# Sparse attention with an MLP: another order of the later batches, another start and other banks at the end

## Chip, core and metric

The kernel runs on one core of one Trainium2 chip. The metric is the device time of one execution in microseconds. Most executions of one kernel on one core fall into one state here ("fast"), and only those are compared. TensorE is named PE, VectorE DVE, ScalarE ACT, GpSimd POOL and SyncE SP in the profile; PEld is TensorE's weight load.

## The reference

Four batches, eight heads, 768 positions, head size 64. Scores are masked by blocks of 32 (neighbours, first and last block, three sampled blocks per row), go through a softmax and meet the values; the result, as rows of 512, goes through an MLP with a squared relu.

```python
scores = scale * np.matmul(q, k.transpose(0, 1, 3, 2))
scores = np.where(mask, scores, -1000000000.0)
attn = np.exp(scores - np.max(scores, axis=-1, keepdims=True))
attn = attn / (np.sum(attn, axis=-1, keepdims=True) + 1e-09)
x = np.matmul(attn, v)                  # -> (4*768, 512)
r = np.maximum(x @ w_in, 0.0)           # w_in (512, 2048)
out = (r * r) @ w_out                   # w_out (2048, 512)
```

## The kernel before

Two heads make a "pair", so there are 16 pairs, four per batch. A pair's queries are three tiles of 256, its keys three chunks of 256, so there are 144 pieces ("score slots") of scores, exponential and value products. The MLP goes by tiles of 256 or 384 rows: sixteen hidden products, relu on VectorE or ScalarE, square on GpSimd, then output products.

No engine is programmed by hand. Each piece of work is a `Task` with an engine, an assumed duration, a priority and its dependences, and a list scheduler in Python lays them out before the build. What it decides is only the order of instructions on each engine; on the chip they wait for semaphores.

```python
def run_schedule(free, bufs, ring):          # free: when each engine is assumed to start
    ...
            at = min(c[0] for c in cand)
            t = min((c[1] for c in cand if c[0] <= at + 1e-9), key=lambda t: (t.key, t.order))
    ...
order = [(a, qi, cp) for qi in range(NQ) for a in range(HP) for cp in range(CP)]
order += [(u, qi, cp) for u in range(HP, NU) for qi in range(NQ) for cp in range(CP)]
...
need = [mu[b * HP + a, qi] for a in range(HP)        # a hidden tile needs all four pairs
        for qi in range(c0 // QW, (c0 + w - 1) // QW + 1)]
...
def y_pool(T, ts):                           # PSUM bank of an output tile
    return "h" if T == TILES[-1] and ts % 2 else "y"
...
for _ in range(8):                           # warm-up of TensorE's clock
    nc.tensor.matmul(pw, warm[:, 0:P], warm, start=True, stop=True)
...
land_k = [(4.4, 5.0), (7.3,), (9.6,), (12.2,)]       # assumed landing times of the first loads
...
run_schedule({"PE": 4.4, "DVE": 4.3, "ACT": 3.5, "POOL": 7.5, "SP": 10.5}, ...)
```

The softmax here doesn't subtract the row's maximum and nothing guards it: scores larger than these inputs give would overflow.

## Time and profile before

| | |
|---|---|
| time, median of 3 | 324.03 us (323.83 to 324.04) |
| the profiled execution | 325.12 us, span 323.3 us |
| TensorE busy | 308.5 us, 95% of the span |
| ScalarE / VectorE / GpSimd busy | 227.3 / 204.4 / 178.6 us |
| first hidden product | 39.7 us |
| last matmul starts | 319.06 us |

TensorE is busy nearly all the time, so the kernel can win only where TensorE waits or runs slowly.

### The profile page before, as it was taken

The page shows a single profiled execution, that of the slowest core. Times are in us where ns is not written, and L with a number is a line of the kernel's source. Part 1 is how long each engine was busy: PE and PEld are TensorE (multiplying, and loading weights), DVE is VectorE, ACT ScalarE, POOL GpSimd, SP SyncE. Part 2 cuts the span into 40 slices and gives each one's busy share as a digit, 9 for nine tenths or more (in the row PEclk, how much of TensorE's full clock was granted, in tenths as well). Part 3 has the DMA queues.
Part 4 walks back from the last instruction along what each step waited for, and adds up shares of the span by engine and source line. Part 5 has one row for each costly group of instructions (what it writes and reads, how often), then busy time and mean ns, then how long its engine had stood idle before and what let it go on. Part 6 is the DMA issues. An engine that isn't in the chain of part 4 may idle for free. (4 is left out here: it accounts for less than half of the span.)

```text
span 323.3 us, 6147 instructions
## 1 busy us (share of the span) xinstructions
PE 308.5 (95%) x2333; PEld 173.9 (54%) x2333; DVE 204.4 (63%) x367; ACT 227.3 (70%) x362; POOL 178.6 (55%) x226
## 2 busy tenths in 40 slices
PE   7998899999999998999989998999999999999994
PEld 2654456556555554555555544565656565555541
DVE  7544463487986877598887695877877653232200
ACT  2698988779998988797768788888788863111211
POOL 7560162287775575097997480554545455666620
PEclk9999999999999999999999999999999999999999
DMA  7997199416555734843754712000000000100002
GB/s 245 325 209 169 48 128 185 146 26 203 86 179 160 220 87 152 229 109 120 195 127 126 204 32 71 16 0 34 32 2 32 35 29 35 36 32 32 34 32 97
DMA packets 42453, 34.47 MB, mean 107 GB/s; under 512 B 20664, under 2 KB 39352, under 8 KB 42424
## 3 DMA queue, kind: packets, MB, share of 16 engines
q1 hardware_dynamic: 37656, 29.63, 32.1%
q0 software_dynamic: 4224, 4.19, 7.9%
q8 instruction: 18, 0.29, 0.4%
q10 hardware_dynamic: 544, 0.26, 0.3%
q14 instruction: 11, 0.09, 0.1%
HBM read 27.26 MB, written 6.29 MB: 104 GB/s over the span
## 5 line engine op out<-in xcount | busy, mean ns | idle before, releaser
L437 POOL TENSOR_TENSOR g<-r 128x384 bf16<-128x384 f32 (+1 forms) x144 | 129.4, 908 | 113.0 <-DVE r L431 91.2
L365 ACT ACTIVATE pT<-ps 128x1024 bf16<-128x1024 f32 x144 | 143.2, 1018 | 31.9 <-PE ps L359 23.1
L420 PE MATMUL ph<-xT,w_in_sb 128*128 128x384 bf16 (+1 forms) x576 | 118.5, 309 | 1.0 <-DVE r L431 0.9
L450 PE MATMUL py<-w_out_sb,g 128*128 128x512 bf16 x384 | 109.1, 379 | 1.4 <-ACT ys L455 1.4
L370 DVE TENSOR_TENSOR pT<-pT,mask 128x1024 bf16<-128x1024 bf16 x108 | 89.2, 839 | 18.3 <-ACT pT L365 16.8
L431 DVE TENSOR_SCALAR r<-ph 128x384 f32<-128x384 f32 (+1 forms) x98 | 49.6, 512 | 54.3 <-PE ph L420 42.1
L383 PE MATMUL po<-pT,VA 128*128 128x256 bf16 x288 | 71.9, 276 | 5.6 <-ACT pT L365 3.7
L420 PEld LDWEIGHTS <-w_in_sb 128*128 128x128 bf16 x576 | 53.0, 98 | 44.8 <-issue 11.2
L385 PE MATMUL po<-pT,VB 128*128 128x256 bf16 x288 | 71.4, 274 | 0.0
L450 PEld LDWEIGHTS <-g 128*128 128x128 bf16 x384 | 37.1, 98 | 25.3 <-issue 2.5
L359 PE MATMUL ps<-QT,KT 64*128 64x256 bf16 x576 | 50.6, 275 | 0.0
L383 PEld LDWEIGHTS <-VA 128*128 128x128 bf16 x288 | 28.2, 98 | 29.7 <-issue 15.4
L429 ACT ACTIVATE r<-ph 128x384 f32<-128x384 f32 (+1 forms) x46 | 20.7, 450 | 27.7 <-POOL g L437 20.2
L359 PEld LDWEIGHTS <-KT 64*128 64x128 bf16 x576 | 22.6, 95 | 21.6 <-issue 19.4
L385 PEld LDWEIGHTS <-VB 128*128 128x128 bf16 x288 | 28.4, 98 | 6.3
L455 ACT COPY ys<-py 128x512 f32<-128x512 f32 x24 | 13.9, 584 | 18.5 <-PE py L450 14.8
L403 DVE TENSOR_TENSOR xT<-po,rs 64x256 bf16<-64x256 f32 x48 | 19.8, 413 | 11.3 <-ACT rs L394 11.2
L392 ACT ACTIVATE ls<-po 64x256 f32<-64x256 f32 x48 | 18.3, 382 | 7.1 <-PE po L385 6.1
L297 POOL CAST qc<-qs 128x768 bf16<-128x768 f32 (+1 forms) x20 | 16.1, 812 | 10.8 <-DMA qs<-in_q_dram 8.4
L394 ACT ACTIVATE rs<-ls 128x256 f32<-128x256 f32 x48 | 20.0, 416 | 1.5
L404 DVE TENSOR_TENSOR xT<-po,rs 64x256 bf16<-64x256 f32 x48 | 20.5, 428 | 0.6
L393 ACT ACTIVATE ls<-po 64x256 f32<-64x256 f32 x48 | 18.1, 376 | 0.6
(49 smaller groups left out, 109.9 us busy)
## 6 DMA issues: line engine op xcount, KB each, us to landing
vs<-in_v_dram SPq DMA_DIRECT2D x16, 384.0 KB, 4.8
out_dram<-ys SPq DMA_DIRECT2D x24, 256.0 KB, 2.0
ks<-in_k_dram SPq DMA_DIRECT2D x15, 384.0 KB, 4.6
qs<-in_q_dram SPq DMA_DIRECT2D x12, 384.0 KB, 3.6
w_in_sb<-in_moe_w_in_dram POOLq DMA_DIRECT2D x4, 512.0 KB, 8.7
w_out_sb<-in_moe_w_out_dram POOLq DMA_DIRECT2D x4, 512.0 KB, 9.4
qs<-in_q_dram SPq DMA_DIRECT2D x11, 128.0 KB, 5.4
ks<-in_k_dram SPq DMA_DIRECT2D x1, 256.0 KB, 2.9
```

The lines of the kernel that those rows point to most:

```text
L359: nc.tensor.matmul(ps[:, h, c, :], KT[i][hs, ksl[c]], QT[i][hs, qsl], start=not add, stop=True, skip_group_check=True)
L365: nc.scalar.activation(out=pT, in_=stile.pop((u, qi, cp)), func=AF.Exp, scale=scale)
L370: eng.tensor_mul(out=pT, in0=pT, in1=mask[:, None, qi, cp * 2:cp * 2 + 2, :].broadcast_to([P, 2, 2, QW]))
L383: nc.tensor.matmul(po[:, 0, :], VA[i][:, n, :], pT[:, 0, c, :], start=first, stop=last, skip_group_check=True)
L385: nc.tensor.matmul(po[:, 1, :], VB[i][:, n, :], pT[:, 1, c, :], start=False, stop=last, skip_group_check=True)
L394: nc.scalar.activation(out=rs, in_=ls, func=AF.Exp, scale=-1.0)
L404: V.tensor_mul(out=xT[b][D:P, a, qsl], in0=po[D:P, 1, :], in1=rs[D:P, :])
L420: nc.tensor.matmul(ph, w_in_sb[:, kc, f * P:(f + 1) * P], xT[b][:, kc, c0:c0 + w], start=(kc == 0), stop=(kc == KM - 1))
L429: nc.scalar.activation(out=r, in_=htile.pop((T, f)), func=AF.Relu)
L431: V.tensor_scalar(out=r, in0=htile.pop((T, f)), scalar1=0.0, scalar2=None, op0=AOP.max)
L437: G.tensor_mul(out=g, in0=r, in1=r)
L450: nc.tensor.matmul(py, gtile[T, f][:, ts * P:(ts + 1) * P], w_out_sb[:, f, :], start=(f == 0), stop=(f == NF - 1))
```

## The change

Three parts are meant to help: the order, the start and the end. In batches 1 to 3, query tiles 0 and 1 of all four pairs come first and tile 2 after, so that a batch's first hidden tile (rows 0 to 383) is ready earlier. At the start, one load goes to another queue, the mask's constants are made in two parts and as 16-bit numbers, and of the eight warm-up matmuls of 512 columns four stay, while ten of 256 columns are put between the first real ones. The last three output tiles get a bank each, and the last one's copy and store are cut in two. With the start, the times that the scheduler assumes change too.

```diff
-    load_part(nc.scalar, 0, 0, 0, 1)
+    load_part(nc.sync, 0, 0, 0, 1)
...
-    for _ in range(8):
-        nc.tensor.matmul(pw, warm[:, 0:P], warm, start=True, stop=True)
+    for _ in range(4):
+        warm_up(512)
...
-    key = consts.tile([P, S], F32, name="key")
+    key = consts.tile([P, S], mybir.dt.int16, name="key")
...
-    one_hot()
+    one_hot(0, 2)
...
-        return "h" if T == TILES[-1] and ts % 2 else "y"
+        return "h" if T == TILES[-1] and ts else "y"
...
+    def out_last(T, ts):
+        py = ytile.pop((T, ts))
+        for eng, queue, half in ((nc.scalar, nc.scalar, 0), (V, nc.sync, 1)):
...
-    land_k = [(4.4, 5.0), (7.3,), (9.6,), (12.2,)]
+    land_k = [(3.0, 4.4), (6.7,), (9.3,), (12.0,)]
...
-    order += [(u, qi, cp) for u in range(HP, NU) for qi in range(NQ) for cp in range(CP)]
+    for b in range(1, B):
+        for qs in (range(NQ - 1), range(NQ - 1, NQ)):
+            order += [(u, qi, cp) for u in range(b * HP, (b + 1) * HP) for qi in qs for cp in range(CP)]
...
+    wu = [Task("PE", 0.2, 1e6, (lambda: warm_up(256)), get=None if i else "po") for i in range(10)]
...
-    run_schedule({"PE": 4.4, "DVE": 4.3, "ACT": 3.5, "POOL": 7.5, "SP": 10.5},
+    run_schedule({"PE": 3.0, "DVE": 3.9, "ACT": 3.2, "POOL": 6.2, "SP": 10.5},
```

More of the change, by code (lines that the diff above doesn't have):

```diff
@@ L218, with warm_up @@
     pw = ps_o.tile([P, 512], F32, name="pw", tag="po")
-    for _ in range(8):
-        nc.tensor.matmul(pw, warm[:, 0:P], warm, start=True, stop=True)
+    def warm_up(n):
+        nc.tensor.matmul(pw[:, 0:n], warm[:, 0:P], warm[:, 0:n], start=True, stop=True)
+    for _ in range(4):
+        warm_up(512)
     HALVES = (slice(0, D), slice(D, P))
-    key = consts.tile([P, S], F32, name="key")
+    key = consts.tile([P, S], mybir.dt.int16, name="key")
     ends = consts.tile([P, 2], F32, name="ends")
@@ L229, with one_hot @@
         G.iota(ends[hs, 0:1], pattern=[[0, 1]], base=0, channel_multiplier=block, **small)
-    G.iota(key, pattern=[[1, NCH], [NCH, P]], base=0, channel_multiplier=0, **small)
+    G.iota(key[:, 0:2 * P], pattern=[[1, 2], [NCH, P]], base=0, channel_multiplier=0, **small)
     identb = consts.tile([P, P], BF, name="identb")
     make_identity(nc, identb)
-    def one_hot():
-        V.tensor_scalar(out=ends[:, 1:2], in0=ends[:, 0:1], scalar1=float(block - 1), scalar2=None, op0=AOP.add)
-        V.tensor_scalar(out=oh, in0=key, scalar1=ends[:, 0:1], scalar2=None, op0=AOP.is_ge)
-        V.scalar_tensor_tensor(out=oh, in0=key, scalar=ends[:, 1:2], in1=oh, op0=AOP.is_le, op1=AOP.mult)
+    G.iota(key[:, 2 * P:S], pattern=[[1, NCH - 2], [NCH, P]], base=2, channel_multiplier=0, **small)
+    def one_hot(n0, n1):
+        cols = slice(n0 * P, n1 * P)
+        V.tensor_scalar(out=oh[:, cols], in0=key[:, cols], scalar1=ends[:, 0:1], scalar2=None, op0=AOP.is_ge)
+        V.scalar_tensor_tensor(out=oh[:, cols], in0=key[:, cols], scalar=ends[:, 1:2], in1=oh[:, cols],
+                               op0=AOP.is_le, op1=AOP.mult)
     sbf = consts.tile([nb, n_rand], F32, name="sbf")
@@ L251 @@
     V.memset(pm[:, 0, nb - 1:nb], 1.0)
-    one_hot()
+    V.tensor_scalar(out=ends[:, 1:2], in0=ends[:, 0:1], scalar1=float(block - 1), scalar2=None, op0=AOP.add)
+    one_hot(0, 2)
+    bm = consts.tile([nb, 2, D], BF, name="bm")
+    V.memset(bm, 0.0)
     V.tensor_copy(out=sbf, in_=sb_i.rearrange("q (r two) -> q r two", two=2)[:, :, 0])
@@ L258 @@
         cur = 1 - cur
-    bm = consts.tile([nb, P], BF, name="bm")
-    V.memset(bm, 0.0)
-    for hs in HALVES:
-        V.tensor_scalar(out=bm[:, hs.start:hs.start + nb], in0=pm[:, cur, :], scalar1=-1.0, scalar2=-NEG,
-                        op0=AOP.add, op1=AOP.mult)
+    V.tensor_scalar(out=bm[:, :, 0:nb], in0=pm[:, cur:cur + 1, :].broadcast_to([nb, 2, nb]), scalar1=-1.0,
+                    scalar2=-NEG, op0=AOP.add, op1=AOP.mult)
     bq = consts.tile([P, S], BF, name="bq")
@@ L271, in rows_product @@
         pb = ps_y.tile([P, QW], F32, name="pb", tag="y")
-        nc.tensor.matmul(pb, bm, oh[0:nb, qi * QW:(qi + 1) * QW], start=True, stop=True)
+        nc.tensor.matmul(pb, bm.rearrange("a t j -> a (t j)"), oh[0:nb, qi * QW:(qi + 1) * QW], start=True, stop=True)
         mtile[qi] = pb
@@ L454, in out_copy @@
         ys = work.tile([P, d_model], F32, name="ys", tag="ys", bufs=3)
-        nc.scalar.copy(out=ys, in_=ytile.pop((T, ts)))
+        py = ytile.pop((T, ts))
         ystile[T, ts] = ys
+        nc.scalar.copy(out=ys, in_=py)
     def store(T, ts):
         nc.sync.dma_start(out=ov[T[0], :, T[1] // P + ts, :], in_=ystile.pop((T, ts)))
+    def out_last(T, ts):
+        py = ytile.pop((T, ts))
+        for eng, queue, half in ((nc.scalar, nc.scalar, 0), (V, nc.sync, 1)):
+            ys = work.tile([P, d_model], F32, name="ys", tag="ys", bufs=3)
+            cols = slice(half * d_model // 2, (half + 1) * d_model // 2)
+            (eng.copy if eng is nc.scalar else eng.tensor_copy)(out=ys[:, cols], in_=py[:, cols])
+            queue.dma_start(out=ov[T[0], :, T[1] // P + ts, cols], in_=ys[:, cols])
     for u in (2, 3):
@@ L475 @@
     K_PARTS = {0: [(0, 1), (1, CP)]}
-    land_k = [(4.4, 5.0), (7.3,), (9.6,), (12.2,)]
-    land_q = [(4.4, 13.8, 15.2), (7.5, 14.1, 15.5), (9.8, 14.5, 15.9), (12.4, 14.8, 16.2)]
-    land_v = [6.2, 8.6, 11.0, 13.4]
+    land_k = [(3.0, 4.4), (6.7,), (9.3,), (12.0,)]
+    land_q = [(3.5, 13.8, 15.3), (7.1, 14.2, 15.7), (9.7, 14.6, 16.1), (12.4, 14.9, 16.5)]
+    land_v = [5.6, 8.2, 10.9, 13.5]
     LAT = 0.08
@@ L490 @@
     wl, tr, gate, mk, tp = {}, {}, [], {}, {HP - 1: []}
+    wu = [Task("PE", 0.2, 1e6, (lambda: warm_up(256)), get=None if i else "po") for i in range(10)]
+    for a, b in zip(wu, wu[1:]):
+        b.deps.append(a)
+    wu[0].bufs[0].holds += 1
+    wu[-1].put.append(wu[0].bufs[0])
+    oh_t = Task("DVE", 1.0, 0.5, (lambda: one_hot(2, NCH)), after=5.6, **SEM)
     rc = []
     for qi in range(NQ):
-        rp = Task("PE", 0.2, -7 + 7 * qi, (lambda qi=qi: rows_product(qi)), get="y", **pe)
-        rc.append(Task("ACT", 0.4, -7 + 7 * qi, (lambda qi=qi: rows_copy(qi)), deps=[rp], put=[rp], **SEM))
+        rp = Task("PE", 0.2, -7 if qi == 0 else 12 * qi - 6, (lambda qi=qi: rows_product(qi)), get="y",
+                  deps=[oh_t] if qi else [], after=7.0 * qi, **pe)
+        rc.append(Task("ACT", 0.4, -7 if qi == 0 else 12 * qi - 6, (lambda qi=qi: rows_copy(qi)), deps=[rp], put=[rp], **SEM))
     for qi in range(NQ):
@@ L559, in attend @@
         sc = Task("PE", 0.42 if len(slots) == 1 and s >= N_FIRST else 0.645, s, (lambda: scores(slots)),
-                  deps=[rc[qi] for u, qi, cp in slots if qi < NQ_ADD and u < HP] + [ev[u][1, cp] for u, qi, cp in slots] + [ev[u][0, qi] for u, qi, cp in slots] + sc_all[-1:],
+                  deps=[t for u, qi, cp in slots if qi < NQ_ADD and u < HP for t in (rc[qi], oh_t)[:1 + (cp > 0)]] + [ev[u][1, cp] for u, qi, cp in slots] + [ev[u][0, qi] for u, qi, cp in slots] + sc_all[-1:],
                   get="ps", n=len(slots), **pe)
@@ L624 @@
                     yhead = yy
-                if part == NY - 1:
+                if part == NY - 1 and T_ == TILES[-1] and last_ts:
+                    Task("ACT", 0.59, 0, (lambda T_=T_, ts=ts: out_last(T_, ts)), deps=[yy], get="ys",
+                         put=[yhead], late=2.0)
+                elif part == NY - 1:
                     yc = Task("ACT", 0.59, 0, (lambda T_=T_, ts=ts: out_copy(T_, ts)), deps=[yy], get="ys",
```

## The prediction

> **What bounds the kernel now.** I read the page's first part, the busy time by stretches, the waits of TensorE after 40 us, and the timeline of both ends. Columns of the stretches: start:end, length, then busy us (and instructions) of PE, PEld, DVE, ACT, POOL, then granted clock, DMA share, GB/s.
>
> ```profile
> PE 308.5 (95%) x2333; PEld 173.9 (54%) x2333; DVE 204.4 (63%) x367; ACT 227.3 (70%) x362; POOL 178.6 (55%) x226
> ...
> 24.00:32.00 8.00, 6.40 (x72) 3.68 (x74) 3.58 (x10) 7.16 (x10) 0.12 (x1) 1.00 0.76 165
> ...
> 120.00:140.00 20.00, 18.52 (x140) 10.10 (x138) 13.44 (x24) 16.57 (x28) 7.09 (x8) 1.00 0.55 165
> ...
> 180.00:200.00 20.00, 18.78 (x139) 10.10 (x134) 14.31 (x24) 16.18 (x26) 9.94 (x10) 1.00 0.38 106
> ...
> 240.00:260.00 20.00, 20.00 (x150) 11.65 (x148) 14.67 (x26) 16.63 (x26) 9.66 (x9) 1.00 0.08 27
> ```
>
> TensorE bounds the kernel from 40 us on and ScalarE before that (7.16 of 8 us at 24 to 32 us, with no hidden-layer matmul yet). TensorE has no room from 220 to 315 us; it starves a little in two stretches, 120 to 140 and 180 to 200 us.
>
> ```profile
> PE po L383 <- ACT pT L365: 1.4, 3, 0.7
> PE po L383 <- DVE xT L404: 1.4, 3, 0.9
> PE ph L420 <- DVE r L431: 0.9, 1, 0.9
> ```
>
> These are only gaps in which no matmul is in flight. From the start times of consecutive matmuls less their streaming time (0.11 us for 256 columns, 0.16 for 384, 0.22 for 512) I count every pause above 0.25 us between 40 and 311 us. The sum is 7.1 us: 2.0 at 122 to 133 us, 1.0 at 164, 2.7 at 191 to 204, the rest in four pauses of 0.3 to 0.4 us before 76 us. The first and third places are where one batch's MLP has only output matmuls left and the next batch's first hidden tile is not ready.
>
> The start, as a timeline (start, length, engine, line, instruction):
>
> ```profile
> 2.33 0.62 DVE L236 TENSOR_SCALAR oh<-key,ends 128x768 bf16<-128x768 f32 x1
> ...
> 2.98 1.02 DVE L237 SCALAR_TENSOR_TENSOR oh<-key,ends,oh 128x768 bf16<-128x768 f32 x1
> ...
> 5.15 0.26 DVE L262 TENSOR_SCALAR bm<-pm 24x24 bf16<-24x24 f32 x2
> ...
> 5.47 0.39 PE L272 MATMUL pb<-oh,bm 24*128 24x256 bf16 x1 [0.69 <-DVE bm L262]
> ...
> 12.48 0.42 PE L383 MATMUL po<-pT,VA 128*128 128x256 bf16 x1
> ...
> 12.69 0.42 PE L385 MATMUL po<-pT,VB 128*128 128x256 bf16 x1
> ...
> 14.17 2.12 ACT L365 ACTIVATE pT<-ps 128x1024 bf16<-128x1024 f32 x2 [1.92 <-PE ps L359]
> ...
> 15.38 0.27 PE L383 MATMUL po<-pT,VA 128*128 128x256 bf16 x1
> ...
> 15.49 0.27 PE L385 MATMUL po<-pT,VB 128*128 128x256 bf16 x1
> ```
>
> Equal matmuls start 0.21 us apart at 12.5 us and 0.11 apart at 15.4: TensorE runs at half rate until about 13.3 us, although the granted-clock column says 1.00. Its slow transposes and value products hold back the fourth exponential to 14.17, ScalarE's last long wait; after that ScalarE has bubbles of only 0.3 us until 40 us. So what the start is worth is read at that fourth exponential.
>
> The end:
>
> ```profile
> 314.70 1.07 ACT L455 COPY ys<-py 128x512 f32<-128x512 f32 x2 [6.33 <-PE py L450]
> 315.83 3.61 PE L450 MATMUL py<-w_out_sb,g 128*128 128x512 bf16 x16 [0.78 <-ACT ys L455]
> ...
> 319.52 0.59 ACT L455 COPY ys<-py 128x512 f32<-128x512 f32 x1 [3.75 <-issue]
> ```
>
> The last output product waits 0.78 us for its PSUM bank; then come copy, store and 3.2 us to the end of the span.
>
> **What the Trainium skill says.** "TensorE: Matmul & The Clock Gate", Part 1: the array runs at half rate by default and goes to full rate after about 3.4 us of sustained work, counted in a free-running window. The trace agrees on the factor (0.21 against 0.11 us). Eight warm-up matmuls of 0.43 us (1.19 to about 4.6 us) plus the gapped work up to 9.9 us did not release it, the dense work of 9.9 to 13.3 us did; that fits windows that end near 6.5, 9.9 and 13.3 us, which is my inference. "DMA: Bandwidth & Descriptors", Issuing engines are not separate DMA queues: issuing from another engine saves only issue time. The trace agrees: the DMA share is 1.04 or more from 3.1 us on, so moving the first query load to the SP queue changes order, not bandwidth. "PSUM — Partial Sum Buffer", Terms: ScalarE and VectorE may not access one bank and quadrant at once. No run shows this yet, but the built program does what it implies: the new VectorE half copy of the last tile waits for ScalarE's half copy.
>
> **Part 1, the start.** The one-hot work ahead of the mask rows falls from 768 to 256 columns. The first compare took 0.62 us; with about 0.15 fixed (the 128x1 instruction before it), a third of the rest gives 0.31. The second took 1.02, 0.2 of it fixed, so about 0.47. That saves 0.31 + 0.55 = 0.85, one write of bm instead of two about 0.13: bm and all casts come about 1.0 us earlier (first product near 4.4 instead of 5.47). But the program order puts six 256-column warm-ups directly behind it: 6 x 0.213 = 1.28 us cold, so the first transposes start near 5.9, as before (5.83). The warm-ups eat this head start. What they buy is a nearly gapless TensorE: following the order with cold durations, three more warm-ups to 7.0, transposes to 7.4, scores, one warm-up, row product, scores to 9.75, that is about 3.1 us streaming of the 3.4 between 6.5 and 9.9, against about 2.6 before. So I expect the full rate at about 9.9 instead of 13.3. Then the first exponential is near 8.5 (8.76 before), the second near 10, third 11, and the fourth, for pair 1, whose keys are cast near 8.4 and transposed at full rate near 9.8, at about 12.1 instead of 14.2. ScalarE is the bound from there, so the gain is carried to 40 us: 2.1 us. If the clock is not released it is only 0.2 to 0.5. I weight these and take **1.8 us**. The second one-hot part (about 0.46 + 0.74 us on VectorE) lies in its wait for transposes and costs the second scores product little.
>
> **Part 2, the order.** Nothing is added: the same 144 score, 144 value, 576 hidden and 384 output pieces; the groups of scores between other matmuls (each costs about 0.2 us of switching, from starts at 59.81, 60.02, 60.34) go from 107 to 108: **+0.2**. A batch's first hidden tile needs query tiles 0 and 1 of four pairs: 8/12 of the batch's attention now, 11/12 before. In the built order hidden matmuls issued by score slot 72, 84, 108, 120 are 188, 212, 320, 350 before and 196, 252, 334, 376 after. The two starved places of before (slots 72 to 84: 24 hidden pieces; 108 to 114: 4) are gone; a shorter one (slots 66 to 72: 6) is new, with eight output pieces to fill it. Of 7.1 us I let 4.7 (both batch boundaries) go, and put 1.0 back for the new place: **3.7 us** gained.
>
> **Part 3, the end.** The third tile gets its own bank: **-0.78**. The last copy, 0.59, becomes ScalarE's half (0.37, as the 128x256 PSUM copy of the mask rows) and, behind it because of the wait, VectorE's half (0.42, as its 128x256 relu) plus about 0.1 for the semaphore: 0.89, so 0.3 later; the half store may land 0.1 to 0.2 sooner (2.0 us for 256 KB). Net **+0.2**.
>
> Sum: 324.03 - 1.8 - 3.7 - 0.78 + 0.2 + 0.2 = 318.1 us, 1.8% less.
>
> **Rivals.** (a) The warm-ups fail: the window's phase is other than inferred, or 92% busy is not enough, and they only delay the transposes. For it: three microseconds of dense warm-up failed before. Then about 319.7. (b) The pauses move rather than go: K and V buffers of a pair now live until the third query tile, there are five, and loads, casts and transposes of the next pairs bunch; or ScalarE limits the runs of scores without hidden work. Against it: a buffer is free at least 15 score slots (about 2 us each) before reuse, and a load plus transpose takes 4.8 + 2.9 us. Then the middle gives 1 us, total about 320.8. (c) The middle becomes gapless: all 7.1 us go with the new place hidden by its output matmuls, and the total is near 314.7. (d) TensorE was the bound anyway and an early start is absorbed: against it, the idle 10% of 24 to 40 us come from ScalarE, and later work follows in the same order.
>
> **Range and chances.** Best case of start and middle together 315, both poor about 321.5. The limit for 2% is 317.55, 0.5 below my number, so faster is a little less likely than not. Nothing adds time worth 2%. Range 315.3 to 321.0; faster 0.40, same 0.59, slower 0.01.
>
> **What would show it.** Right: 256-column matmuls 0.11 us apart from about 10 us; fourth exponential near 12.1; first hidden matmul near 38 instead of 39.7; TensorE busy over 19.3 in each 20 us stretch between 120 and 200 us except one; no wait before the last sixteen output matmuls; the VectorE half copy beginning only after ScalarE's. Wrong: half rate still at 13 us; new pauses on DMA transposes or VectorE in the third-tile passes; more than 3 pauses over 0.5 us after 60 us.

## The result and the profile after

The changed kernel takes 320.65 us (median of 4, 320.05 to 321.18) against 323.98 for before. The ratio is 0.9898 (95% interval 0.988 to 0.9915), 1.0% less time. A ratio here is the mean time of one kernel's fast runs over that of the other's in the same rounds, so not quite the ratio of the medians quoted.

The page's first part and the busy time by stretches, in the columns told in the prediction:

```profile
PE 306.7 (96%) x2339; PEld 174.2 (55%) x2339; DVE 203.3 (64%) x369; ACT 226.7 (71%) x362; POOL 176.9 (55%) x227
...
24.00:32.00 8.00, 7.24 (x79) 4.04 (x78) 3.23 (x7) 7.44 (x11) 0.00 (x0) 1.00 0.69 145
...
120.00:140.00 20.00, 19.34 (x152) 11.00 (x150) 16.66 (x27) 16.04 (x25) 15.82 (x17) 1.00 0.54 153
...
180.00:200.00 20.00, 18.56 (x137) 10.27 (x136) 15.29 (x27) 16.48 (x27) 11.37 (x13) 1.00 0.47 124
```

The first starved stretch is better (19.34 us busy of 20, before 18.52). The second is not (18.56, before 18.78). TensorE's waits after 40 us:

```profile
PE ph L426 <- DVE r L437: 1.6, 4, 0.7
PE po L389 <- ACT pT L371: 0.9, 3, 0.4
PE py L456 <- ACT ys L463: 0.7, 1, 0.7
```

One line of the same view of the kernel before, which the prediction left out, belongs beside the last of these:

```profile
PE py L450 <- ACT ys L455: 1.4, 2, 0.8
```

So output products waited for their bank twice before, at 193 us and at the end; the second of these waits has gone. The wait of hidden products for VectorE's relu has grown from one of 0.9 us to four with 1.6 in total. By the count of the prediction (start times of consecutive matmuls less streaming, pauses above 0.25 us after 40 us), but this time from every single matmul record, pauses went from 6.6 us, plus 0.9 for the last bank, to 5.1. Two of the new kernel's largest, in the timeline (start, length, engine, line, instruction):

```profile
127.88 1.18 DVE L303 CAST qc<-ks 128x768 bf16<-128x768 f32 x1
...
129.09 0.56 DVE L437 TENSOR_SCALAR r<-ph 128x384 f32<-128x384 f32 x1
...
129.71 0.48 PE L426 MATMUL ph<-xT,w_in_sb 128*128 128x384 bf16 x2 [0.66 <-DVE r L437]
...
184.84 0.58 ACT L463 COPY ys<-py 128x512 f32<-128x512 f32 x1 [0.17 <-PE py L456]
...
185.48 1.89 PE L456 MATMUL py<-w_out_sb,g 128*128 128x512 bf16 x8 [0.67 <-ACT ys L463]
```

At 129 us VectorE runs a 1.18 us cast of the next pair's keys before the relu that TensorE needs. At 185 us eight output products wait for a copy out of the one bank that such tiles have in mid-kernel, as they did at 193 us before. The start:

```profile
2.22 0.28 DVE L241 TENSOR_SCALAR oh<-key,ends 128x256 bf16<-128x256 int16 x1
...
2.54 0.48 DVE L242 SCALAR_TENSOR_TENSOR oh<-key,ends,oh 128x256 bf16<-128x256 int16 x1
...
4.20 0.20 DVE L268 TENSOR_SCALAR bm<-pm 24x48 bf16<-24x48 f32 x1
...
4.77 1.46 PE L221 MATMUL pw<-warm 128*128 128x256 bf16 x6
...
11.47 0.27 PE L391 MATMUL po<-pT,VB 128*128 128x256 bf16 x1
...
11.58 0.27 PE L389 MATMUL po<-pT,VA 128*128 128x256 bf16 x1
...
14.08 1.02 ACT L371 ACTIVATE pT<-ps 128x1024 bf16<-128x1024 f32 x1 [0.51 <-PE ps L365]
```

The constants take what the prediction worked out (0.28 and 0.48 us; 0.31 and 0.47 were expected), and equal matmuls are 0.11 us apart by 11.5 us. The fourth exponential starts at 12.55 us, the sixth at 16.25 (before 17.44). The end:

```profile
311.82 1.07 ACT L463 COPY ys<-py 128x512 f32<-128x512 f32 x2 [6.33 <-PE py L456]
315.71 0.37 ACT L474 COPY ys<-py 128x256 f32<-128x256 f32 x1 [2.81 <-issue]
...
316.11 0.42 DVE L474 COPY ys<-py 128x256 f32<-128x256 f32 x1 [10.25 <-ACT ys L474]
```

The bank's wait is gone, and VectorE's half copy starts 0.03 us after ScalarE's has ended.

### The profile page after: what moved, and what is told of

Its sections match the earlier page's. It is cut to its first block, busy times and chain, and to the rows that moved or that the text cites. A ratio compares the mean times of both kernels' runs of the same rounds, so it can differ in the third digit from the quotient of the medians.

```text
span 319.4 us, 6150 instructions
## 1 busy us (share of the span) xinstructions
PE 306.7 (96%) x2339; PEld 174.2 (55%) x2339; DVE 203.3 (64%) x369; ACT 226.7 (71%) x362; POOL 176.9 (55%) x227
## 4 chain that ended last, share of the span: by engine, by line
PE 81%; ACT 9%; DVE 6%; issue 4%; DVEq 0%; ACTq 0%
PE ph L426 24%; PE py L456 22%; PE po L389 11%; PE ps L365 10%; PE po L391 9%; ACT pT L371 5%; PE ps L361 3%; DVE pT L376 2%; DVE r L437 1%; ACT ls L399 1%; ACT ls L398 1%; ACT rs L400 1%; PE pw L221 1%; PE pt L314 1%; DVE xT L410 0%
## 5 line engine op out<-in xcount | busy, mean ns | idle before, releaser
L398 ACT ACTIVATE ls<-po 64x256 f32<-64x256 f32 x48 | 18.2, 380 | 8.6 <-PE po L391 7.6
L463 ACT COPY ys<-py 128x512 f32<-128x512 f32 x23 | 13.3, 584 | 12.7 <-PE py L456 12.7
L303 POOL CAST qc<-qs 128x768 bf16<-128x768 f32 (+1 forms) x20 | 15.2, 771 | 11.8 <-DMA qs<-in_q_dram 10.1
L308 POOL CAST VA<-vs 128x384 bf16<-128x384 f32 x16 | 10.8, 672 | 16.9 <-PE po L389 9.4
```

Of the source, the lines that this page charges most:

```text
L398: nc.scalar.activation(out=ls[0:D, :], in_=po[D:P, 0, :], func=AF.Ln)
```

## The experiments

Twelve kernels ran, each on one chip beside the kernel before. All gave right results. Two measures from the traces help, because the times scatter: the start of the 31st exponential (how well the head of the kernel went) and the stretch from there to the start of the last matmul (how well the rest went). Both are start times read from the trace.

| kernel | median us | ratio to before | full clock from, us | 31st exponential | stretch | span after last start |
|---|---|---|---|---|---|---|
| before, first profile | 323.98 | 1 | 13.6 | 52.5 | 266.6 | 4.28 |
| changed | 320.65 | 0.9898 | 10.3 | 51.5 | 263.8 | 4.16 |
| changed, again | 320.72 | 0.9907 | 10.7 | 51.7 | 263.7 | 4.13 |
| order only | 320.94 | 0.9895 | 4.4 to 7.8, 11.2 | 51.45 | 263.0 | 4.26 |
| start only | 325.3 | 1.0034 | 9.0 | 51.0 | 268.5 | 4.26 |
| end only | 322.77 | 0.9959 | 5.0 to 8.5, 11.9 | 51.4 | 265.4 | 4.13 |
| changed, ten warm-ups out | 320.73 | 0.9892 | 12.0 | 51.7 | 263.8 | 4.14 |
| order and end | 319.24 | 0.9852 | 4.8 to 8.2, 11.7 | 51.3 | 262.1 | 4.12 |
| changed, old planner times | 319.82 | 0.9876 | 10.3 | 52.3 | 262.2 | 4.15 |
| before, new planner times | 325.01 | 1.0038 | 13.0 | 52.2 | 267.4 | 4.26 |
| order and end, again | 319.12 | 0.9851 | 5.1 to 8.5, 11.9 | 51.4 | 262.05 | 4.12 |
| order and end, delay 0.10 | 319.88 | 0.9878 | 13.2 | 52.3 | 262.7 | 4.15 |
| order and end, delay 0.06 | 319.83 | 0.9864 | 4.5 to 7.9, 11.3 | 51.1 | 261.8 | 4.13 |
| order and end in halves | 318.75 | 0.9845 | 4.6 to 8.0, 11.4 | 51.0 | 262.2 | 3.61 |

The 95% intervals of the ratios are about 0.002 to 0.003 wide on each side, 0.6 to 1.0 us.

The executions also differ in when the clock was released, and the record tells part of that for the timed ones. A half-rate window after an early full-rate one leaves a mean granted clock of 0.992 to 0.995; 1.000 means only that no half-rate window is on record. "Order only" and the kernel before ran in both ways: medians 320.2 against 323.8 us at 0.994 to 0.995, and 321.4 against 324.7 at 1.000. So the order's gain, 3.2 to 3.6 us, does not come from how the start fell out.

**Each part alone.** The kernel before with the lines of one part. "Order only" takes the `order` hunk, "end only" the banks and `out_last`, "start only" all the rest of the diff, the planner's times among it.

```diff
 # order only
-    order += [(u, qi, cp) for u in range(HP, NU) for qi in range(NQ) for cp in range(CP)]
+    for b in range(1, B):
+        for qs in (range(NQ - 1), range(NQ - 1, NQ)):
+            order += [(u, qi, cp) for u in range(b * HP, (b + 1) * HP) for qi in qs for cp in range(CP)]
```

> The kernel before with only the new order of the later batches. Theory from the two traces: pauses of TensorE between 40 and 311 us fall by about 1.5 to 2 us, so 2.0 us faster than before (ratio 0.994). The prediction's term says 3.7 us faster (0.9886). Rival: the order gains nothing by itself and the whole gain is start and end (ratio 1.000).

It gave 0.9895, 3.4 us of 324.4: the prediction's term, not the 2.0 us that I had read from the two traces after the result. The stretch is 266.6 before and 263.0 here.

> The changed kernel with the old order of the later batches and the old end, so only loads, constants and warm-ups differ from before. Theory from the two traces: full rate near 10.3 us, sixth exponential 1.2 us earlier, total 1.0 us faster (ratio 0.997). The prediction's term says 1.8 us (0.9944). Rival: an early start is absorbed by TensorE's later schedule and gives 0 to 0.3 us.

It gave 1.0034 (1.0014 to 1.0054): 1.1 us slower. None of the three expectations holds. The head was good (31st exponential at 51.0 us), but the stretch is 268.5 us, 1.9 more than before, although no instruction after the first 20 us is new. So I put the loss down to the order that the scheduler laid out for the rest; this run alone does not show it, and two kernels below test it.

> The kernel before with only the third bank for the last outputs and the split last copy. Theory: the 0.9 us pause before the last sixteen output products goes; the split changes the last copy and store by less than 0.2 us: 0.7 to 1.0 us faster (ratio 0.997 to 0.998). Rival: the split also halves the last copy and the store, 1.2 us faster or more (0.996).

It gave 0.9959 (0.9941 to 0.9977), 1.3 us. Its trace shows 1.1 us of it: the 0.94 us pause before the last sixteen products is gone and the span ends 0.15 us sooner after the last matmul starts. The interval holds both the theory (0.997) and the rival (0.996), so the times do not decide between them; in the trace the split last copy brings no more than the 0.15.

The three ratios alone add up to 3.4 - 1.1 + 1.3 = 3.6 us; the whole change brought 3.3 and, on another chip, 3.0.

**The warm-ups.** The list of ten `wu` tasks is taken out of the changed kernel.

```diff
-    wu = [Task("PE", 0.2, 1e6, (lambda: warm_up(256)), get=None if i else "po") for i in range(10)]
-    for a, b in zip(wu, wu[1:]):
-        b.deps.append(a)
...
```

> The changed kernel without the ten extra 256-column warm-ups. If they are what releases the clock earlier, full rate comes one window later (near 13.6 us instead of 10.3) while the first transposes and scores come about 1 us earlier; the total is 0.5 to 1.5 us above the changed kernel (ratio to before 0.993 to 0.995). Rival: warm-ups only delay the first transposes, and without them the kernel is as fast or up to 1 us faster than the changed one (ratio 0.987 to 0.990).

It gave 320.73 us and 0.9892; the changed kernel gave 0.9898 and 0.9907. There is no difference to see, as the rival had it. In one trace the full clock came at 12.0 us and not at 10.3, the first exponential at 7.6 and not at 8.7, and by the sixth exponential the two had cancelled (16.45 against 16.25 and 16.46). That the warm-ups caused the earlier release is not shown, since release differs between executions of the same early instructions too.

**The old start with the rest of the change.** "Order and end" is the kernel before plus those two parts.

> The changed kernel unaltered, as the yardstick on this chip: 3.3 us faster than before (ratio 0.990). The pauses of TensorE after 40 us should be the same as in its first trace, about 5.1 us above 0.25 us each, and the time of clock release may differ, since it did between traces of identical early code (13.6 us before, two windows earlier in the order-only and end-only runs).

> The kernel before with the new order and the new end, but the old start. Theory (the start's shifted times make the planner lay out the rest anew and bring back pauses): the pauses stay near the 2.8 us of the order-only run, and the kernel is 4.5 to 5 us faster than before (ratio 0.985), 1 to 1.5 us faster than the changed kernel. Rival (start is a small gain as measured in exponentials, 0.4 us): it is 0.4 us slower than the changed kernel, ratio 0.991.

The changed kernel repeated: 0.9907, and its ten pauses stood at the same places with the same lengths within 0.03 us (sum 5.06, first 5.08). "Order and end" gave 0.9852 (0.9825 to 0.988), 1.5 us below the changed kernel's median. Its pauses sum up to 2.75 us, and the two starved stretches are full:

```profile
120.00:140.00 20.00, 20.00 (x151) 11.48 (x150) 17.35 (x28) 16.40 (x27) 15.21 (x17) 1.00 0.56 168
180.00:200.00 20.00, 20.00 (x148) 11.39 (x147) 16.21 (x26) 17.21 (x29) 13.93 (x14) 1.00 0.59 159
```

So the order does what it was meant to do as long as the start is the old one, and with the new start 1.5 us of its 3.4 are lost again. The same trace shows the clock, in stretches cut where it changed (this view has PE's busy time, the clock, the DMA share and GB/s):

```profile
1.41:4.83 3.42, 3.38 (x8) 1.00 0.80 243
4.83:8.24 3.41, 2.13 (x19) 1.00 0.99 328
8.24:11.65 3.41, 3.41 (x28) 0.50 1.07 366
11.65:15.06 3.41, 3.41 (x43) 1.00 1.16 322
```

The eight old warm-ups filled the window that ended at 4.83 us, and TensorE ran at full rate for one window, then at half rate for one, then at full rate. The kernel before in its first profile, with the same early instructions, was at half rate until 13.6 us. (In the first of these four stretches the column says 1.00, but it stands there before any clock record; the matmuls were 0.43 us apart, half rate.)

**Instructions or plan.** The changed kernel with the planner's old `land_*` times and engine start times, and the kernel before with the new ones. Not one instruction is added or removed, only their order differs.

```diff
 # changed, old planner times (the other kernel is the reverse)
-    land_k = [(3.0, 4.4), (6.7,), (9.3,), (12.0,)]
+    land_k = [(4.4, 5.0), (7.3,), (9.6,), (12.2,)]
...
-    run_schedule({"PE": 3.0, "DVE": 3.9, "ACT": 3.2, "POOL": 6.2, "SP": 10.5},
+    run_schedule({"PE": 4.4, "DVE": 4.3, "ACT": 3.5, "POOL": 7.5, "SP": 10.5},
```

> The changed kernel, but the planner is given the old landing times and the old start times of the engines; instructions are the same, only their order may differ. Theory (new plan, not new work, costs the middle): pauses after 40 us differ from 5.1 us by more than 1 us, in either direction, and the time moves by the same amount. Rival (the warm-ups and loads themselves cost the middle): pauses within 0.5 us of 5.1 and the time within 0.5 us of the changed kernel.

> The kernel before, but the planner is given the changed kernel's landing times and start times; no instruction is added or removed. Theory (new plan, not new work, made the start-only kernel slower): pauses after 40 us rise from 6.6 (without the bank's) to 8 or more and the time by 1 to 2 us (ratio 1.003 to 1.006). Rival: ratio 1.000 within 0.0015, so the loss of the start-only kernel lies in its instructions.

The changed kernel with old times: pauses 3.8 us instead of 5.1, stretch 262.2 instead of 263.7, time 319.82 instead of 320.72, although its head is 0.6 us worse (31st exponential at 52.3). Its stretch is also that of "order and end" (262.1), which has the old start's instructions. So the longer stretch of the changed kernel comes from the plan that the new times draw, not from its instructions. The kernel before with new times: 1.0038 (1.0008 to 1.0069), slower, with a stretch of 267.4 instead of 266.6. But its pauses are 6.65 us without the bank's and did not rise to 8; that half of the expectation failed, and where those 0.8 us are I did not find. Nor do its times show a loss clearly: all six runs have a granted clock of 1.000, and against three runs of before with 1.000 the medians differ by only 0.6 us (325.0 and 324.4). And 0.8 is less than the 1.9 us that "start only" lost; whether the rest came from its new tasks in the plan or from their execution was not separated.

**Is any new plan worse, or these times?** Two tiny changes of the planner alone, in "order and end", beside a repetition.

```diff
-    LAT = 0.08
+    LAT = 0.10      # the other kernel: 0.06
```

> The kernel before with new order and new end, unaltered, as the yardstick on this chip: about 4.6 us faster than before (ratio 0.985 to 0.987), pauses after 40 us again 2.75 us at the same places, and 262.1 us from the start of the 31st exponential to that of the last matmul. If the places repeat while clock release differs, pauses belong to the order of instructions and not to the chip's state.

> The same, but the planner assumes 0.10 us instead of 0.08 for a semaphore's delay: the same instructions in another order, with nothing changed at start or end. Theory (any change of the planner's times draws a new plan, and its pauses fall out by luck): from the 31st exponential to the last matmul differs from 262.1 us by 0.5 us or more. Rival (the changed kernel's new pauses come from its start itself): within 0.4 us of 262.1.

> The same with 0.06 us for the semaphore's delay. Theory: again another plan, the stretch from the 31st exponential to the last matmul off 262.1 us by 0.5 us or more, up or down. Rival: within 0.4 us.

The repetition gave the same pauses (2.76 us) and the same stretch within 0.01 us. With 0.10 us the stretch grew by 0.7, with 0.06 it shrank by 0.2. So a change of 0.02 us in one assumption can cost 0.7 us, and it needn't. The theory held for one kernel and the rival for the other. The new start times lengthened the stretch in both pairs that differ in them alone (1.6 and 0.8 us), which is more than these two trials did, though 0.8 is hardly more than 0.7; whether they are worse than other changes, and why, stays open.

**A better end.** In "order and end" the last output tile is made in two banks of 256 columns, one half in sixteen matmuls after the other, so that the first half is copied and stored beside the second half's products.

```diff
+    def last_half(T, ts, part):
+        half, step = divmod(part, NY // 2)
+        if step == 0:
+            pool, tag = (ps_o, "po") if half else (ps_h, "h")
+            ytile[T, ts, half] = pool.tile([P, d_model // 2], F32, name="py", tag=tag)
...
```

> New order and third bank, and the last output tile made in two banks of 256 columns each, first one half in sixteen matmuls and then the other, so that ScalarE's copy and store of the first half run beside the products of the second, and VectorE's copy needs not wait for ScalarE's. In the changed kernel the last matmul starts 4.15 us before the end of the span; here the wait for ScalarE's half (0.37 + 0.03 us) should go and the last matmul is 0.11 us shorter, so 3.6 to 3.75 us. Total about 0.4 us below the yardstick, within the noise of the times. Rival: loading 16 more weights at 256 columns slows the last products and eats it.

The last matmul starts 3.61 us before the span's end instead of 4.16, within what was expected. The two half copies no longer stand behind each other:

```profile
311.79 0.37 ACT L460 COPY ys<-py 128x256 f32<-128x256 f32 x1 [1.10 <-issue]
...
313.55 0.42 DVE L460 COPY ys<-py 128x256 f32<-128x256 f32 x1 [9.90 <-PE py L452]
```

With 318.75 us and 0.9845 (0.9823 to 0.9866) it is the fastest kernel, 1.6% below before. Its lead over "order and end" is 0.5 us at the end of the trace. Between the medians it is 0.4, within the noise; between the runs with a granted clock of 0.995 alone it is 0.5 (318.7 and 319.1, four runs and three).

## Why the prediction was right, and where it was not

The time, 320.65 us, lies in the range of 315.3 to 321.0, and the class, within 2%, was the likelier one. But the number was 2.5 us too low, and one of the three terms had the wrong sign: that the range still held the result, 0.35 us from its upper end, is in part luck.

**Part 2, the order (3.7 us less 0.2).** Right in mechanism and size for what it described: the order alone brings 3.4 us. (The 7.1 us of pauses it started from are 0.5 too many: the matmul records give 2.2 and not 2.7 us for 191 to 204 us.) In the changed kernel this gain is not whole. The prediction said that the starved places of before are gone and put 1.0 us back; in the changed kernel one is there again at 185 us and relu waits have come, and the pauses fell by only 1.5 us. With the old start they fell by 3.8. The place at 185 us could have been read from the built order: between score slots 101 and 104 it issues ten output matmuls and no hidden one (320 hidden ones at both), and the prediction took its counts at slots 66 to 84 and 108 to 120 only. Its sign of TensorE being busy over 19.3 us in all stretches but one came true all the same (19.34, 19.82, 19.60, 18.56).

**Part 1, the start (1.8 us).** This is the step that failed; alone it costs 1.1 us. It failed in two places. First, "TensorE runs at half rate until about 13.3 us" was taken for a property of the kernel. It belonged to that execution and some others. Of nine traces with the old early instructions (one of them in another order), six had a full-rate window from 4.4 to 5.1 us on and the final release by 11.9 us, and the 31st exponential then starts at 51.0 to 51.5 us; in the other three, release came at 13.0 to 13.6 and that exponential at 52.2 to 52.5. The changed kernel's two traces have it at 51.5 and 51.7, no better than the good case of before. The steps in between were right (constants 1.0 us sooner, warm-ups eat that, release near 9.9: it was 10.3), and the fourth exponential came at 12.55, 0.45 late. The fifth then waited for scores till 14.08, so that from the sixth on 1.2 us of lead remained over an unlucky trace, and nothing over a lucky one. (The trace of "start only", released at 9.05 us, had 51.0 at the 31st, as the best of the lucky ones.) Second, "the gain is carried to 40 us" left out what follows: a changed start changes the planner's times, and with them the order of every later instruction. That cost 1.6 us of stretch in the changed kernel, by the run with the old planner times.

**Part 3, the end (0.78 less 0.2).** The bank's pause was 0.94 us by start times, and the half copies stood behind each other as expected, 0.03 us apart. But the end came 0.12 us sooner, not 0.2 later, after the last matmul starts (4.16 against 4.28 us). The copies did end 0.23 us later after that start (1.28 against 1.05); what was sized too small is the gain behind them, 2.87 us from the last copy's end to the end of the span against 3.23, 0.36 us and not 0.1 to 0.2. The Trainium skill's page "PSUM — Partial Sum Buffer", Terms, was the reason given for that order of copies, and the trace agrees with it in that the copies do not overlap; two banks removed the wait.

Of the rivals, (a) and (b) were each half right. The ten warm-ups brought nothing (320.73 us without them), although full rate did come near 10 us with them. Pauses in part moved rather than went, at 129 us by a relu behind a cast on VectorE, not by transposes. Of the signs named, first hidden matmul near 38 us failed (39.1), and five pauses of 0.5 us or more after 60 us were the sign of "wrong" that came true.

## What to carry to other kernels

Compare the time of the profiled execution with the timed ones before reading small things from its trace: here it was 1.1 us slow, and the 1.8 us predicted for the start rested on mending that one execution's bad luck. Where a program lays out the order of instructions from assumed times, a change at the start is a change everywhere, so try each part alone and give the planner its old times as a control. When two engines must empty one PSUM bank one after the other, split the products into two banks and let the first half leave beside the second.

## What the Trainium skill lacked or had wrong

- "TensorE: Matmul & The Clock Gate", Part 1, describes free-running windows of about 3.4 us, and the traces agree on their length (3.41 us between changes). The page has no threshold of how busy a window must be, and the profile's busy time gives none. With windows counted back from the final release, in "before, new planner times" one with TensorE busy 3.25 of 3.41 us (6.16 to 9.57 us) was followed by half rate and the next, busy 3.15, by full rate; in "order and end, delay 0.10" one busy for all of its 3.41 us (6.38 to 9.79 us) was followed by half rate. Its table gives half rate after an idle window; in "order and end" a window busy 2.13 of 3.41 us was followed by half rate. (Elsewhere the page tells of half rate coming back through short idle times, without a share.)
- The same page speaks of a transition that varies by 500 ns between runs. Here, with the same early instructions in the same order, final release came at 11.2 to 11.9 us in six traces and at 13.2 and 13.6 in two, and the start of the 31st exponential differed by 1.5 us. A note further down that page, which calls the number of slow matmuls variable from run to run, fits better.
- No page that I read says that the profile's granted clock can read 1.00 ahead of the first clock record, though the same page warns that such records can be unreliable. In the first profile it did so up to 13.6 us while matmuls ran at half rate, 0.21 us apart for 256 columns.
